# Cosine attention, Fourier mixing and a feed-forward block: a lone tile first, other homes for one batch's raw rows, and a new priority table

## The chip, the cores and the metric

The kernel runs on one core of a Trainium2 chip. The metric is the device time of one execution in microseconds. The kernel before takes 575.24 us (median of three runs, 574.73 to 575.60).

## The reference

Eight batches of twelve heads, 448 tokens, 64 numbers a head. Queries and keys are divided by their norms, the scores by tau, the softmax weights the values. Then a real-valued two-dimensional Fourier transform over tokens and over the 768 channels is added to its input, each row is normalised, and a feed-forward block of 768 to 3072 to 768 with a relu is added:

```python
def _attn_ref(q, k, v, tau) -> np.ndarray:
    q_n = q / (np.linalg.norm(q, axis=-1, keepdims=True) + 1e-06)
    k_n = k / (np.linalg.norm(k, axis=-1, keepdims=True) + 1e-06)
    scores = np.matmul(q_n, k_n.transpose(0, 1, 3, 2)) / tau
    scores = scores - np.max(scores, axis=-1, keepdims=True)
    attn = np.exp(scores)
    attn = attn / (np.sum(attn, axis=-1, keepdims=True) + 1e-09)
    return np.matmul(attn, v).astype(np.float32)

def _moe_ref(x, w_ch1, w_ch2) -> np.ndarray:
    X = np.fft.fft(x, axis=1)
    X = np.fft.fft(X, axis=2)
    mixed = np.real(X).astype(np.float32)
    u = x + mixed
    mu = np.mean(u, axis=-1, keepdims=True)
    var = np.mean((u - mu) ** 2, axis=-1, keepdims=True)
    un = (u - mu) / np.sqrt(var + 1e-06)
    ch = np.maximum(un @ w_ch1, 0.0) @ w_ch2
    return (u + ch).astype(np.float32)
```

All inputs and the output are float32; q, k and v are batch by head by token by channel.

## The kernel before

**Work and its names.** Everything below is written as a list of operations, each with a name that ends in its batch. For a batch the loads `ld_k`, `ld_q` (and `ld_t`, the last 64 tokens) bring raw rows from DRAM; `sq` squares them, `ss` sums the squares, `ln` and `nrm` make the norms of a group of heads (an Ln and an Exp on ACT, L1173 and L1175), `sc` scales the rows, and they reach the TensorE's layout (batches 0 and 1 through TensorE transposes `tk`, `tq`, `tt` and copies; the others through DMA transposes `tr`, L1393). `qk` are the score products (L1464 and L1477), `ex` the exponentials on ACT (L1442), `pv` the products with V (L1495 for the last tokens, L1501), `x` the division. `f`, `fs`, `te` and `fd` belong to the Fourier transform, `ba`, `bs`, `ln2` and `rs` to the row norm (`bs` is L1769), `tru` brings the normed rows to TensorE's layout by DMA (L1800; in batch 0 `tn` by TensorE, L1789, and `eu` copies them out of PSUM, L1797). `h0` to `h23` are the 24 column blocks of the first feed-forward product (L1864), `relu` takes four blocks of one tile or two of a pair out of PSUM (L1880), and `y` or `m1` to `m7` are the second product (L2008), `fin` the additions behind it, `st` the store.

**Tiles.** Rows of the feed-forward block are worked in tiles of 128. Even batches have three tiles, odd ones four (28 in all), and two tiles that follow each other make a pair whose second product is done with seven block products instead of eight (L2073 on: sums and differences of the two weights and of the two hidden tiles). `ONES` on L27 names the two tiles that stay single: (batch, tile) (0, 0) and (2, 2). Batch 7 and part of batch 6 multiply the first weight in the same way (`ups`, L1959, with the weight sums on VectorE at L1901, L1912 and L1944).

**Order.** Each operation gets a priority, to which a table `SHIFT` adds a number of its own, and a table `HOME` ties some operations to an engine. `Plan.schedule` (L675 on) then plays the program through with costs from tables, always starting the operation with the lowest priority among those that could start first, and so fixes one list of instructions for each engine. On the chip each engine runs its list strictly in that order, waiting where a row has a wait; the DMA issues of SP and of POOL stand in those lists too. `Plan.fill` then puts warm-up products (six matmuls on data of no interest, L2258) where the schedule has holes on TensorE: with the identity up to the first `h`, with a piece of W1 from there to 20 us ahead of the planned end, the latter only where the schedule is thin.

**Batch 1's raw rows.** `first_norm` (L1179) loads the rows of batches 0 and 1. Batch 0's stand in the tile buffers TX. Batch 1's come in two groups of three head pairs: `ld_k0_1`, `ld_t0_1`, `ld_q0_1` and `ld_k1_1`, `ld_t1_1`, `ld_q1_1`; a K or Q load is 576 KB, a t load is two of 96 KB. They all lie where W2 will be (`W2b[:, 10:24]`), and the squares of the first group's Q lie there as well (`W2b[:, 7:10]`, square `sqQ0_1`); W2's pieces therefore wait for the operations that read them (L2235 to L2241). Nothing in W2b is old, so these loads wait only for the first piece of W1 (gate, `self.w[0]`).

**Head of the program.** W1 comes on POOL's DMA queue in seven pieces and W2 behind it in twelve, each piece behind the landing of an earlier one (L1145). The first tile of batch 0 is single: 24 blocks `h` of 6 matmuls with 128 columns, in groups of four that share one of two PSUM banks, so `h8` can start once `relu0` has read the bank of `h0` to `h3`.

Of the kernel before, what the change touches and what calls it, by code (L numbers as in the profile page):

```python
# [26 lines left out]
ONES = ((0, 0), (2, 2))  # L27
# [55 lines left out]
    "iota": {0: -4743.9411}, "iotak": {0: -3749.0012}, "cst": {0: 2295.738}, "iotad": {0: 1504.4864}, "rown": {0: 3564.9514},  # L83
    "tqd": {0: 5876.6502, 1: 5614.4443}, "trd": {0: 5875.7288}, "tpd": {0: -1558.5233, 1: 550.4848}, "tad": {0: 4737.392},
    "tqs": {0: 4545.6213, 1: 5636.9779}, "trs": {0: 4448.6198}, "tps": {0: -162.6304, 1: -1607.3824}, "tas": {0: -178.9521}, "ktd0": {0: 1975.3204},
# [4 lines left out]
    "mask": {0: 35657.0228}, "sinp": {0: 48649.0823}, "half": {0: 440.6683, 1: 3500.6271}, "sinn": {0: 17464.9799}, "ldt": {0: 44319.0778},  # L90
# [2228 lines left out]
```

## Time and profile before

| what | value |
|---|---|
| median of three runs | 575.24 us (574.73 to 575.60) |
| the profiled execution | 575.0 us, span 573.2 us |
| TensorE (PE) busy | 553.7 us, 97% of the span |
| VectorE (DVE), ScalarE (ACT), GpSimd (POOL) busy | 434.0, 392.9, 224.4 us |
| granted TensorE clock | 1.00 |
| DMA | 62.19 MB, 108 GB/s on average |

The profiled execution is 575.0 us long, 1.8 us more than its span. "Busy" counts the time in which an engine runs an instruction; TensorE's warm-up products count as busy, though they do nothing for the result. The page cuts the span into 40 slices of 14.3 us.

### The profile page before, as it was taken

The page shows a single profiled execution, that of the slowest core. Times are in us where ns is not written, and L with a number is a line of the kernel's source. Part 1 is how long each engine was busy: PE and PEld are TensorE (multiplying, and loading weights), DVE is VectorE, ACT ScalarE, POOL GpSimd, SP SyncE. Part 2 cuts the span into 40 slices and gives each one's busy share as a digit, 9 for nine tenths or more (in the row PEclk, how much of TensorE's full clock was granted, in tenths as well). Part 3 has the DMA queues.
Part 4 walks back from the last instruction along what each step waited for, and adds up shares of the span by engine and source line. Part 5 has one row for each costly group of instructions (what it writes and reads, how often), then busy time and mean ns, then how long its engine had stood idle before and what let it go on. Part 6 is the DMA issues. An engine that isn't in the chain of part 4 may idle for free.

```text
span 573.2 us, 16025 instructions
## 1 busy us (share of the span) xinstructions
PE 553.7 (97%) x6616; PEld 432.9 (76%) x6616; DVE 434.0 (76%) x923; ACT 392.9 (69%) x734; POOL 224.4 (39%) x332
## 2 busy tenths in 40 slices
PE   3899999999999899999999999999999999999998
PEld 2578887686787687878778688687886876959695
DVE  9889868987469867986789669965679379886353
ACT  7998976576776885578648886686665761948171
POOL 8522414356328542702380736443524003041304
PEclk9999999999999999999999999999999999999999
DMA  9999997976359645963496569461691200132001
GB/s 213 170 241 202 164 195 108 163 173 111 111 82 113 158 88 111 155 145 70 95 157 76 99 138 125 105 140 23 136 87 27 72 2 17 42 48 66 24 34 56
DMA packets 183945, 62.19 MB, mean 108 GB/s; under 512 B 166688, under 2 KB 181664, under 8 KB 183872
## 3 DMA queue, kind: packets, MB, share of 16 engines
q1 hardware_dynamic: 129824, 38.35, 35.2%
q0 software_dynamic: 54048, 22.81, 32.1%
q8 instruction: 52, 0.85, 0.6%
q14 instruction: 21, 0.17, 0.1%
HBM read 51.90 MB, written 11.01 MB: 110 GB/s over the span
## 4 chain that ended last, share of the span: by engine, by line
PE 78%; DVE 8%; ACT 6%; issue 3%; POOL 2%; DMA 2%; SPq 1%; POOLq 0%; DVEq 0%; ACTq 0%
PE PS L1864 28%; PE PS L2008 26%; PE PS L1959 7%; PE PS L1501 5%; PE PS L1464 5%; PE PS L1495 2%; PE PS L1477 1%; DMA TX<-in_q_dram 1%; ACT F L1769 1%; POOL QH L1387 1%; DVE F L1547 1%; POOL OUTB L2034 1%; PE PS L1685 1%; DVE OUTB L2045 1%; DVE X L1521 1%
## 5 line engine op out<-in xcount | busy, mean ns | idle before, releaser
L1864 PE MATMUL PS<-UNT,W1b 128*128 128x256 bf16 (+1 forms) x1728 | 185.4, 264 | 0.3 <-DVE UNT L1797 0.2
L1442 ACT ACTIVATE E<-PS 128x900 bf16<-128x900 f32 (+1 forms) x192 | 148.7, 827 | 30.3 <-PE PS L1464 24.3
L1864 PEld LDWEIGHTS PS<-UNT,W1b 128*128 128x128 bf16 x1728 | 153.4, 98 | 20.1 <-issue 1.9
L2008 PE MATMUL PS<-W2b,HQ 128*128 128x384 bf16 x720 | 124.9, 326 | 0.0
L1387 POOL TENSOR_TENSOR QH<-STG,SM 128x256 bf16<-128x256 f32 x126 | 84.4, 696 | 86.8 <-DVE SM L1177 65.0
L2008 PEld LDWEIGHTS PS<-W2b,HQ 128*128 128x128 bf16 x720 | 68.8, 98 | 43.1 <-issue 0.4
L2034 POOL TENSOR_TENSOR OUTB<-OUTB,U 128x192 f32<-128x192 f32 x72 | 51.6, 737 | 118.2 <-ACT OUTB L2029 115.6
L2008 PE MATMUL PS<-TX,HQ 128*128 128x384 bf16 (+2 forms) x444 | 76.4, 322 | 0.9 <-DVE OUTB L2045 0.5
L1880 ACT ACTIVATE HQ<-PS 128x512 bf16<-128x512 f32 x86 | 51.2, 595 | 28.8 <-PE PS L1864 27.6
L2108 DVE TENSOR_TENSOR HQ<-HQ 128x1536 bf16<-128x1536 bf16 (+1 forms) x73 | 54.1, 744 | 12.2 <-ACT HQ L1880 7.0
L2008 PEld LDWEIGHTS PS<-TX,HQ 128*128 128x128 bf16 x444 | 41.5, 98 | 27.9 <-DVE OUTB L2045 2.4
L1374 ACT ACTIVATE QH<-STG 128x384 f32<-128x384 f32 x84 | 43.1, 519 | 17.6 <-DVE SM L1376 11.6
L1376 DVE TENSOR_REDUCE SM<-QH 128x6 f32<-128x384 f32 x84 | 45.3, 544 | 11.3 <-ACT QH L1374 11.0
L1501 PE MATMUL PS<-VB,E 128*128 128x65 bf16 x1152 | 51.6, 193 | 0.0
L2067 POOL DMA_INDIRECT out_dram<-OUTB,IDX x21 | 23.7, 1127 | 69.2 <-DVE OUTB L2045 43.4
L1501 PEld LDWEIGHTS PS<-VB,E 128*128 128x128 bf16 x1152 | 47.8, 97 | 1.3
L1880 DVE TENSOR_SCALAR HQ<-PS 128x512 bf16<-128x512 f32 x40 | 27.4, 685 | 23.9 <-PE PS L1864 23.8
L1495 PE MATMUL PS<-VZ,E 128*128 128x130 bf16 x192 | 41.6, 219 | 2.0 <-issue 1.9
L1727 DVE SCALAR_TENSOR_TENSOR U<-ACG,X 128x768 bf16<-128x768 f32 (+4 forms) x39 | 39.5, 1023 | 0.9
L2029 ACT ACTIVATE OUTB<-PS 128x384 f32<-128x384 f32 x36 | 17.7, 491 | 32.2 <-PE PS L2008 29.4
L1464 PE MATMUL PS<-QK 64*128 64x225 bf16 (+2 forms) x864 | 39.2, 227 | 0.5 <-ACT QK L1290 0.5
L1464 PEld LDWEIGHTS PS<-QK 64*128 64x128 bf16 x864 | 25.6, 95 | 13.2 <-issue 6.6
(195 smaller groups left out, 784.5 us busy)
## 6 DMA issues: line engine op xcount, KB each, us to landing
STG<-in_q_dram SPq DMA_DIRECT2D x18, 384.0 KB, 3.9
STG<-in_k_dram SPq DMA_DIRECT2D x18, 384.0 KB, 3.9
VB<-in_v_dram POOLq DMA_DIRECT2D x24, 192.0 KB, 6.4
W2b<-in_moe_w_ch_dram POOLq DMA_DIRECT2D x12, 384.0 KB, 7.4
W1b<-in_moe_w_ch_dram POOLq DMA_DIRECT2D x5, 768.0 KB, 14.7
out_dram<-OUTB SPq DMA_DIRECT2D x7, 384.0 KB, 2.7
W2b<-in_k_dram SPq DMA_DIRECT2D x2, 576.0 KB, 9.1
W2b<-in_q_dram SPq DMA_DIRECT2D x2, 576.0 KB, 15.9
```

Of the source, the lines that this page charges most:

```text
L1374: P.add("act", lambda a, sq=sq, src=buf[:, w * x:w * x + w]: a.activation(sq, src, ACTF.Square), t_act(w), pr, f"sq{i}_{b}", reads=bn, wri ...
L1376: P.add("dve", lambda v, o=SS[:, i, H // ns * x:H // ns * (x + 1)], sq=sq: v.tensor_reduce(o, sq.rearrange("p (h d) -> p h d", d=DH), AX.X ...
L1387: r = v.tensor_tensor(v3(qh)[:, h:h + 4], v3(buf)[:, h:h + 4], RN[:, i, h:h + 4].unsqueeze(2).to_broadcast((128, 4, DH)), AluOp.mult)
L1442: return a.activation(o, self.PS[:, bk:bk + nc_, 0:SQ2], ACTF.Exp, scale=1.0 / self.tau)
L1464: i = pe.matmul(self.PS[:, bk + h, c0:c0 + n], self.KT[r, jj, kt * 128:(kt + 1) * 128], self.QT[r, jj, cols], start=True, stop=True)
L1495: r = pe.matmul(o, st(6), self.VZ[:, j, :], start=not split, stop=(split and i == 0), skip_group_check=True)
L1501: r = pe.matmul(o[:, 65 * h:65 * h + 65], st(2 * kt + h), self.VB[:, kt, 2 * j + h, :], start=(split and i == h == kt == 0), stop=((not sp ...
L1864: r = pe.matmul(self.PS[:, bk, x * n:(x + 1) * n], self.W1b[:, j, ft * 128:(ft + 1) * 128], self.UNT[:, j, cs], start=(j == 0), stop=(j == ...
L1880: return e.activation(o, i, ACTF.Relu) if e is self.nc.scalar else e.tensor_relu(o, i)
L2008: r = pe.matmul(self.PS[:, bk, 0:n], lhs(f), rhs(f), start=(start and f == 0), stop=(stop and f == NF // 2 - 1), skip_group_check=True)
L2034: r = g.tensor_tensor(self.OUTB[:, ob, xs], self.OUTB[:, ob, xs], self.U[:, ut, xs], AluOp.add)
L2108: P.add("dve", lambda v: v.tensor_tensor(cs(o), cs(a), cs(bq), op), 0.16 + 0.3 * len(ks), -0.5, f"{nm}{ks[0]}_{b}", reads=rd, writes=[x fo ...
```

## The change

1. `ONES` is ((0, 0), (2, 0)): batch 2's first tile is the single one and goes first, and its other two make the pair behind it.
2. Batch 1's raw rows no longer lie in W2's home. The first group and the second group's K go to the buffer of batch 0's raw rows (TX, `self.tf[:, 1536:9216]`), the second group's Q and t to the staging buffers STG; the squares of `sqQ0_1` go to the buffer E1 of the exponentials. The loads now also wait for the operations that read batch 0's raw rows (the table `told`), and two of batch 2's loads wait for readers of batch 1's rows in STG. W2's pieces no longer wait for batch 1's rows.
3. The second stretch of warm-up products ends 12 us behind the first `h` instead of 20 us ahead of the planned end.
4. Every number of `SHIFT` and `HOME` is new, so the lists of all engines are in another order.

The program's lists hold the same products otherwise. The diff, of which the tables are left out:

```diff
--- before.py
+++ after.py
@@ -24,7 +24,7 @@
 TF = 4
-ONES = ((0, 0), (2, 2))
+ONES = ((0, 0), (2, 0))
 HELD = (5, 3)
@@ -80,538 +80,556 @@
 SHIFT = {
-    "iota": {0: -4743.9411}, "iotak": {0: -3749.0012}, "cst": {0: 2295.738}, "iotad": {0: 1504.4864}, "rown": {0: 3564.9514},
...
@@ -1198,11 +1216,12 @@
             gate = []
         else:
             cuts = ((0, 3), (3, 6))
-            hf = flat(self.W2b[:, 10:24, :]).bitcast(F32)
-            sw = flat(self.W2b[:, 7:10, :]).bitcast(F32)
+            hf = self.tf[:, 1536:9216].bitcast(F32)
+            sf = flat(self.STG[:])
+            sw = self.E[1][:, 0:2304].bitcast(F32)
             sqs = [[ob[:, 0:1152], sw, ob[:, 1152:1536]], [ob[:, 0:1152], ob[:, 0:1152], ob[:, 1152:1536]]]
             o0 = ["OUT0", "OUT0b", "OUT1", "OUT0d", "OUT1d"]
-            sqn = [[o0, ["SQW"], ["OUT1b", "OUT1d"]], [o0, o0, ["OUT1b", "OUT1d"]]]
+            sqn = [[o0, ["SQW"] + [f"E1_{c}" for c in range(7)], ["OUT1b", "OUT1d"]], [o0, o0, ["OUT1b", "OUT1d"]]]
             qhb = [(qf, 0), (self.tf, 0), (self.tf, 1152)]
             raw = ["Sk0_0", "Sk1_0"]
             qhn = [[["QH0", "QH1x"], raw + ["QM"], raw + ["QMt"]], [["QH1", "QH2"], ["QM"], ["QMt"]]]
@@ -1213,9 +1232,10 @@
         for g, (a, z) in enumerate(cuts):
             n = z - a
             o, ja = 2688 * (a // 3), a % 3
-            K, Q, R = [hf[:, o + x + y * ja:o + x + y * (ja + n)] for x, y in ((0, 384), (1152, 384), (2304, 128))]
+            K, Q, R = [(sf[:, DM + x - 1152 + y * ja:DM + x - 1152 + y * (ja + n)] if b and g and x else hf[:, o + x + y * ja:o + x + y * (ja + n)])
+                       for x, y in ((0, 384), (1152, 384), (2304, 128))]
             nt = (3, 0, 3)[g] if b == 0 else n
-            R3 = hf[:, o + 2304 + 128 * ja:o + 2304 + 128 * (ja + nt)]
+            R3 = R if b else hf[:, o + 2304 + 128 * ja:o + 2304 + 128 * (ja + nt)]
             L = [("k", [(heads(K, n), self.heads(self.k, b, 2 * a, 2 * n, 0, 3, 128, 192))], 0.64 * n),
                  ("q", [(heads(Q, n), self.heads(self.q, b, 2 * a, 2 * n, 0, 3, 128, 192))], 0.64 * n)]
             if nt:
@@ -1225,12 +1245,15 @@
             parts.append((g, a, n, nt, R3, L, [("K", K, [f"Sk{g}_{b}"]), ("Q", Q, [f"Sq{g}_{b}"]), ("T", R, [f"St{gt}_{b}"])]))
         sc, ID = [], self.ID
         for g, a, n, nt, R3, L, ps in parts:
+            told = {}
+            if b:
+                told = {"k": ["Sk1_0", "Sq0_0", "Sq1_0"], "q": ["Sq1_0", "St0_0", "Sk2_0"], "t": ["Sk2_0"]} if g == 0 else {"k": ["Sk2_0", "Sq2_0"]}
             for nm, dm, sv in L:
                 def fn(sy, sem, dm=dm):
                     for dst, src in dm:
                         sy.dma_start(dst, src).then_inc(sem, 16)
                 self.loads.append(P.add("sp", fn, (0.36 if b else 0.55) * len(dm), pg[g], f"ld_{nm}{g}_{b}", writes=[f"S{nm}{g}_{b}"],
-                                        dma=(f"lh{g}{nm}{b}", 16 * len(dm)), serve=sv, after=gate, order=self.loads[-1:] if b == 0 else ()))
+                                        dma=(f"lh{g}{nm}{b}", 16 * len(dm)), serve=sv, after=gate + [r for x in told.get(nm, ()) for r in P.rd[x]], order=self.loads[-1:] if b == 0 else ()))
                 if (b, g, nm) == (0, 1, "k"):
                     self.vgate = self.loads[-1]
             red, rn = [], [[f"RN_{a + j}{i}" for j in range(n)] for i in range(3)]
@@ -1363,7 +1386,7 @@
                 def fn(sy, sem, dm=dm):
                     for dst, src in dm:
                         sy.dma_start(dst, src).then_inc(sem, 16)
-                self.loads.append(P.add("sp", fn, 0.36 * len(dm), pr, f"ld_{kind}{t}_{b}", writes=bn,
+                self.loads.append(P.add("sp", fn, 0.36 * len(dm), pr, f"ld_{kind}{t}_{b}", writes=bn + ({1: ["Sq1_1"], 2: ["Sq1_1", "St1_1"]}.get(s, []) if b == 2 else []),
                                         dma=(key, 16 * len(dm)), after=gate, serve=1.75))
                 r = self.qh_next % 6
                 self.qh_next += 1
@@ -2183,7 +2206,7 @@
         P = self.P
         B = lambda r, c, k: self.W2b[:, 12 * r + 4 * k:12 * r + 4 * k + 4, 384 * c:384 * c + 384]
         X = lambda x, k: self.TX[:, x, 4 * k:4 * k + 4, :]
-        old = ["ID", "rowf", "CSp", "QLt", "QLu", "QLu_1", "QLv", "QLv_1", "QLv_2", "QM", "QMt"] + [f"S{x}{g}_0" for x in "kqt" for g in range(3)] + [
+        old = ["ID", "rowf", "CSp", "QLt", "QLu", "QLu_1", "QLv", "QLv_1", "QLv_2", "QM", "QMt"] + [f"S{x}{g}_0" for x in "kqt" for g in range(3)] + ["Sk0_1", "Sq0_1", "St0_1", "Sk1_1"] + [
             f"QM{t}_{j}" for t in ("", "t") for j in (1, 2)]
         w = lambda r, k: [f"W2_{6 * r + 2 * k + x}" for x in range(2)]
         for k in range(3):
@@ -2235,10 +2258,6 @@
 
                 for c in range(3):
                     self.w[12 + c].deps.update(self.ssk)
-                for c in (3, 4):
-                    self.w[12 + c].deps.add(self.sqw)
-                for c in range(5, 12):
-                    self.w[12 + c].deps.update(self.raw1[3] + (self.raw1[4] if c > 7 else []))
             if b == self.nb - 2:
                 self.s1 = []
                 self.wsums()
@@ -2260,7 +2279,7 @@
                 return fn
             return make
         self.P.fill(7.5, first, self.id_op, warm(self.ID))
-        self.P.fill(first, self.est - 20.0, self.id_op, warm(self.W1b[:, 0, 0:128]), 0.75)
+        self.P.fill(first, first + 12.0, self.id_op, warm(self.W1b[:, 0, 0:128]), 0.75)
         self.P.emit(self.nc, self.es)
         self.es.close()
 
```

**Three places in the lists.** On SP, the loads of batch 1's rows, which stand right behind those of batch 0 (TX<- rows there). A 128x6x192 row is a K or Q load of 576 KB, the two 64x6x64 rows are one t load, d_W1_0 is the landing of W1's first piece, and prog_act, prog_dve and prog_pool stand for a point that ACT, DVE or POOL must have reached. Before:

```order
L1231 DMA W2b<-in_k_dram 128x6x192 [waits d_W1_0]
L1231 DMA W2b<-in_q_dram 64x6x64
L1231 DMA W2b<-in_k_dram 64x6x64
L1231 DMA W2b<-in_k_dram 128x6x192
L1231 DMA W2b<-in_q_dram 128x6x192 x2
L1231 DMA W2b<-in_q_dram 64x6x64
L1231 DMA W2b<-in_k_dram 64x6x64
```

and now:

```order
L1254 DMA STG<-in_q_dram 64x6x64 [waits d_W1_0]
L1254 DMA STG<-in_k_dram 64x6x64
L1254 DMA STG<-in_q_dram 128x6x192
L1254 DMA TX<-in_k_dram 128x6x192 [waits prog_act,prog_dve]
L1254 DMA TX<-in_q_dram 64x6x64 [waits prog_pool,prog_act,prog_dve]
L1254 DMA TX<-in_k_dram 64x6x64
L1254 DMA TX<-in_q_dram 128x6x192
L1254 DMA TX<-in_k_dram 128x6x192 [waits prog_dve,prog_act]
```

Before, the order is k0, t0, k1, q1, q0, t1; now it is t1, q1, k0, t0, q0, k1, so the second group's K moved from third to last, and three of the loads wait for engines.

On ACT, the rows around the first feed-forward products. The 128x1152 squares are `sqK1_1` and `sqQ0_1` (d_lh1k1 and d_lh0q1 are the landings of k1 and q0), UNT<-PS is `eu00_0`, the copy that the first `h` needs, and 128x512 is a `relu`. Before:

```order
L1249 ACTIVATE OUTB<-W2b 128x1152 [waits prog_dve,prog_act,d_lh1k1]
L1769 ACTIVATE F,MV<-U,MV 128x768 [waits prog_dve]
L1797 ACTIVATE UNT<-PS 128x3x128 [waits prog_pe]
L1772 ACTIVATE MV<-MV 128x1 [waits prog_act]
L2206 ACTIVATE CS<-CS 97x2x96 [waits prog_dve]
L1249 ACTIVATE W2b<-W2b 128x1152 [waits d_lh0q1]
L1774 ACTIVATE MV<-MV 128x1 [waits prog_act]
L1880 ACTIVATE TX<-PS 128x512 [waits prog_pe] x2
L1173 ACTIVATE SM<-SM,MV 128x42 [waits prog_dve]
L1175 ACTIVATE SM<-SM 128x42 [waits prog_act]
```

and now:

```order
L1272 ACTIVATE E<-TX 128x1152 [waits d_lh0q1]
L1792 ACTIVATE F,MV<-U,MV 128x768 [waits prog_dve]
L1795 ACTIVATE MV<-MV 128x1 [waits prog_act]
L1820 ACTIVATE UNT<-PS 128x3x128 [waits prog_pe]
L1797 ACTIVATE MV<-MV 128x1 [waits prog_act]
L1272 ACTIVATE OUTB<-TX 128x1152 [waits d_lh1k1]
L1191 ACTIVATE SM<-SM,MV 128x42 [waits prog_dve]
L1193 ACTIVATE SM<-SM 128x42 [waits prog_act]
L2229 ACTIVATE CS<-CS 97x2x96 [waits prog_dve]
L1903 ACTIVATE TX<-PS 128x512 [waits prog_pe]
```

`sqQ0_1` moved from behind `eu00_0` to ahead of it, and `sqK1_1`, the norms of the first group (128x42) and one small copy now stand ahead of the first `relu`.

On TensorE, the place where batch 2's feed-forward block begins and batch 3's first head pair is scored. L2008 (now L2031) are the last products of batch 1's block, 128x225 the scores of batch 3's first pair, 128x130 and 128x65 its products with V, and 128x128 with W1b the blocks `h` of a single tile. Before:

```order
L1464 MATMUL PS<-QK 128x225 x12
L2008 MATMUL PS<-TX,HQ 128x384 x12
L1477 MATMUL PS<-QK,KTD 128x225 x2
L1495 MATMUL PS<-VZ,E 128x130
L1501 MATMUL PS<-VB,E 128x65 x6
```

and now:

```order
L1487 MATMUL PS<-QK 128x225 x12
L2031 MATMUL PS<-TX,HQ 128x384 x12
L1500 MATMUL PS<-QK,KTD 128x225 x2
L1887 MATMUL PS<-UNT,W1b 128x128 x24
L1518 MATMUL PS<-VZ,E 128x130
L1524 MATMUL PS<-VB,E 128x65 x6
```

Four blocks `h` of the single tile, 24 matmuls, came between the scores and the products with V.

More of the change, by code (lines that the diff above doesn't have):

```diff
@@ L82 @@
 SHIFT = {
[L83 to L85 removed]
[4 rows of a table removed]
[L90 removed]
[510 rows of a table removed]
+    "iota": {0: 988.1999}, "iotak": {0: 2280.7807}, "cst": {0: 2561.5506}, "iotad": {0: 3021.5255}, "rown": {0: -5211.4485},
@@ L601 @@
+    "tqd": {0: 7923.068, 1: 60.9428}, "trd": {0: -5147.3146}, "tpd": {0: 13287.2598, 1: 11.7343}, "tad": {0: 13314.1014},
+    "tqs": {0: -5211.7732, 1: 826.4541}, "trs": {0: 55.947}, "tps": {0: -2188.111, 1: -5124.9522}, "tas": {0: 4226.7561}, "ktd0": {0: 3088.7005},
[4 rows of a table added]
+    "mask": {0: 38931.3111}, "sinp": {0: 41339.771}, "half": {0: 3552.1202, 1: 17376.0333}, "sinn": {0: 10202.0605}, "ldt": {0: 53454.3582},
[507 rows of a table added]
 }
 HOME = {
-    "tqd": {0: "dve", 1: "dve"}, "trd": {0: "dve"}, "tas": {0: "act"}, "sinp": {0: "dve"}, "half": {0: "pool", 1: "act"}, "sqK0_0": {0: "act"},
@@ L613 @@
-    "ek1_1": {0: "act"}, "ek2_1": {0: "dve"}, "eq2_1": {0: "act"}, "relu0_0": {0: "act"}, "relu4_0": {0: "act"}, "relu8_0": {0: "dve"},
-    "relu12_0": {0: "act"}, "relu16_0": {0: "act"}
+    "tqd": {0: "dve", 1: "dve"}, "trd": {0: "dve"}, "tad": {0: "dve"}, "tas": {0: "act"}, "sinp": {0: "dve"}, "half": {0: "pool", 1: "act"},
+    "sinn": {0: "act"}, "sqK0_0": {0: "act"}, "sqQ0_0": {0: "act"}, "sqT0_0": {0: "dve"}, "scK0_0": {0: "dve"}, "scQ0_0": {0: "dve"},
+    "scT0_0": {0: "dve"}, "ek0_0": {0: "act"}, "eq0_0": {0: "act"}, "et0_0": {0: "dve", 1: "act"}, "sqK1_0": {0: "dve"}, "sqQ1_0": {0: "act"},
@@ new lines @@
+    "relu10_0": {0: "dve"}, "relu14_0": {0: "act"}, "relu18_0": {0: "dve"}, "relu22_0": {0: "act"}, "ktd2": {0: "dve"}, "gc1_2": {0: "act"},
+    "relu0_1": {0: "act"}, "relu12_1": {0: "act"}, "relu14_1": {0: "act", 1: "dve"}, "relu20_1": {0: "act"}, "relu22_1": {0: "act", 1: "act"},
+    "relu16_1": {1: "dve"}, "relu6_1": {1: "act"}, "ktd3": {1: "act"}, "te0_3": {0: "act"}, "ct0": {0: "dve"}, "ct3": {0: "act"},
+    "relu4_2": {0: "dve"}, "relu16_2": {0: "act", 1: "dve"}, "relu20_2": {0: "dve"}, "relu2_2": {0: "act"}, "relu6_2": {0: "act"},
@@ new lines @@
+    "te0_6": {0: "act"}, "te1_6": {0: "dve"}, "relu0_5": {0: "dve", 1: "dve"}, "relu12_5": {0: "dve"}, "relu16_5": {0: "dve", 1: "act"},
+    "relu6_5": {0: "act", 1: "act"}, "relu18_5": {0: "act"}, "relu8_5": {0: "act"}, "relu10_5": {0: "act"}, "relu14_5": {1: "act"},
+    "ktd7": {0: "act", 1: "act"}, "gc1_7": {0: "act"}, "te0_7": {0: "act"}, "relu0_6": {0: "act"}, "relu12_6": {0: "act"}, "relu2_6": {0: "dve"},
+    "relu14_6": {0: "dve"}, "relu4_6": {0: "dve"}, "relu16_6": {0: "act"}, "relu6_6": {0: "dve"}, "relu18_6": {0: "dve"}, "relu8_6": {0: "dve"},
@@ L615 @@
+    "relu10_6": {0: "act"}, "relu22_6": {0: "act"}, "c2r1_6": {0: "dve"}, "c41_6": {1: "act", 2: "act"}, "c1r1_6": {3: "act"}, "c3r1_6": {3: "act"},
+    "c1r0_7": {1: "act"}, "c2r0_7": {1: "act"}, "c3r0_7": {2: "dve"}, "c40_7": {1: "dve"}, "c1r2_7": {0: "dve", 1: "act"}, "c2r2_7": {0: "dve"},
+    "c42_7": {0: "dve", 1: "act", 2: "dve"}
 }
```

20 lines of the change are left out of this document (12 added, 8 removed), and 1031 rows, old and new, of tables (HOME, SHIFT).

## The prediction

> **What bounds the kernel now.** I read the page's first two parts, then TensorE's waits, then a table of stretches. In the first fence the last three rows are the 40 slices of TensorE and DMA; in the waits the numbers are total us, times and longest.
>
> ```profile
> span 573.2 us, 16025 instructions
> PE 553.7 (97%) x6616; PEld 432.9 (76%) x6616; DVE 434.0 (76%) x923; ACT 392.9 (69%) x734; POOL 224.4 (39%) x332
> PE   3899999999999899999999999999999999999998
> DMA  9999997976359645963496569461691200132001
> ...
> PE PS L2258 <- DVE HQ L1249: 7.6, 1, 7.6
> PE PS L1495 <- issue: 1.9, 2, 1.5
> PE PS L1959 <- DVE HQ L1979: 0.8, 1, 0.8
> PE PS L1959 <- DMA UNT<-F: 0.5, 1, 0.5
> ```
>
> TensorE bounds everything from the second slice on. Its idle time is 573.2 - 553.7 = 19.5 us; 7.6 us of it lie ahead of its first product, and no later wait is longer than 1.5 us. So the change can win little behind the head: the three longest of them hold 1.5 + 0.8 + 0.5 = 2.8 us. The next table gives, for each stretch, its length, the busy us of PE, PEld, DVE, ACT and POOL, the granted clock, the DMA share and GB/s.
>
> ```profile
> 22.00:34.00 12.00, 10.82 (x179) 7.52 (x177) 9.57 (x21) 11.46 (x19) 6.81 (x8) 1.00 1.22 241
> 34.00:48.00 14.00, 13.36 (x192) 10.91 (x188) 12.30 (x39) 13.04 (x19) 1.52 (x2) 1.00 1.18 226
> 48.00:60.00 12.00, 10.90 (x172) 9.95 (x173) 11.74 (x38) 10.34 (x28) 6.05 (x8) 1.00 1.42 184
> 60.00:100.00 40.00, 40.00 (x509) 32.41 (x510) 31.16 (x66) 30.52 (x52) 12.35 (x17) 1.00 1.04 156
> ```
>
> Up to 60 us four things are tight together (ACT is 93 to 96% busy until 48 us, the DMA engines are full); from there TensorE is without a hole. What the change does to the head therefore ends in one number, the time at which that solid stretch begins.
>
> **The head: loads.** The moved rows come on SP's queue while W1 comes on POOL's, both full. These are SP's issues and how long three of them took to land (the large q loads issued at 26.61 and 29.4, and the last t):
>
> ```profile
> 26.61 5.76 SPq L1231 DMA_DIRECT2D W2b<-in_q_dram  x3
> 32.41 5.61 SPq L1231 DMA_DIRECT2D W2b<-in_k_dram  x1
> ...
> L1231 SPq DMA_DIRECT2D W2b<-in_q_dram x2: 1430/1464/1497, 29.4 to 30.9; - x2
> ...
> W2b<-in_q_dram SPq DMA_DIRECT2D x1, 576.0 KB, 14.3
> ...
> W2b<-in_q_dram SPq DMA_DIRECT2D x1, 576.0 KB, 17.4
> ...
> W2b<-in_k_dram SPq DMA_DIRECT2D x1, 96.0 KB, 19.5
> ```
>
> So q1 landed at 26.61 + 14.3 = 40.9, q0 at 29.4 + 17.4 = 46.8 (5.9 us behind q1 in the same queue), and the last byte of batch 1 at 32.41 + 19.5 = 51.9. The same bytes in another order end at the same time if the queue never runs dry. In the new order k1 is last: it lands at about **51.9** (51.4 if the small t loads at the front overlap better), and q0, one large load ahead of the end (5.9 us by these rows, more beside a W1 piece), at 45 to 46.
>
> **The head: ACT.** What stands on ACT there, from the timeline (start, length):
>
> ```profile
> 46.53 0.94 ACT L1769 ACTIVATE F<-U,MV 128x768 bf16<-128x768 bf16 x1 [0.20 <-DVE MV L1765]
> 47.55 0.49 ACT L1797 ACTIVATE UNT<-PS 128x384 bf16<-128x384 f32 x1
> 48.12 0.35 ACT L2206 ACTIVATE CS<-CS 97x192 bf16<-97x192 bf16 x1
> 48.38 1.15 ACT L1249 ACTIVATE W2b<-W2b 128x1152 f32<-128x1152 f32 x1
> 49.72 0.60 ACT L1880 ACTIVATE TX<-PS 128x512 bf16<-128x512 f32 x1
> 51.55 0.32 ACT L1173 ACTIVATE SM<-SM,MV 128x42 f32<-128x42 f32 x1
> 51.91 0.24 ACT L1175 ACTIVATE SM<-SM 128x42 f32<-128x42 f32 x1
> ```
>
> Now `sqQ0_1` waits for q0 ahead of `bs` (L1769) and `eu00`. With q0 at 45.5 the square (1.15) ends at 46.65, and `bs` starts 0.1 later than the 46.53 of its row; with q0 at 45 nothing is late, at 46 it is 0.6. One small operation more stands ahead of the copy, about the 0.24 of the row at 51.91. I take the first `h` **0.3 us later**, at 48.5 (bounds 0 and +0.9).
>
> The other move costs more. `relu0` sits behind `sqK1_1`, hence behind k1: 51.4 to 51.9, then 1.15 + 0.32 + 0.24 + 0.35 + 0.60 = 2.66 by the rows, of which about 0.1 a seam overlaps (48.12 + 0.35 is 48.47 and the next row starts at 48.38): **53.7 to 54.2**. Behind it on ACT stand all later relus and norms of the head. TensorE, in its rows:
>
> ```profile
> 48.17 5.53 PE L1864 MATMUL PS<-UNT,W1b 128*128 128x128 bf16 x96 [0.18 <-DVE UNT L1797]
> 54.14 0.84 PE L2258 MATMUL PS<-W1b 128*128 128x128 bf16 x12 [0.44 <-DVE CS L2207]
> 54.98 1.51 PE L1864 MATMUL PS<-UNT,W1b 128*128 128x128 bf16 x24
> 57.04 0.49 PE L2258 MATMUL PS<-W1b 128*128 128x128 bf16 x6
> ```
>
> Before, 96 matmuls (16 blocks) ran in 5.53 us without a hole, 0.058 us each. Now 48 of them (`h0` to `h7`) end at 48.5 + 2.8 = 51.3 and TensorE then stands until `relu0` is done, **2.4 to 2.9 us**. Before, however, the stretch from 48 to 60 lost 12.00 - 10.90 = 1.1 us to idling and about 1.0 us to three warm-up groups (0.84 - 0.17 + 0.33; those groups are gone now, which alone is worth nothing, since they filled waits). By the time TensorE is past `h23`, batch 1's transposes have long had their data, and these 2.1 us need not be lost again. The head's net is 0.3 + 2.4 - 2.1 = +0.6 with k1 at 51.4 and +1.1 with it at 51.9. I take **+0.6**, since the tight queue also serves W1's pieces and its last 0.5 us may go to them, with bounds -1.5 (rival a) and +2.5 (late end of k1, and most of the old losses paid again).
>
> W2's pieces are freed from waits. That is nothing: the table shows DMA over its full share until 100 us, so an earlier issue only queues. The staging waits of two loads of batch 2 are nothing as well, since in that stretch TensorE is at 40.00 of 40.00 with ACT and DVE at 76 to 78%, cover of several us; if that cover were gone a late row would cost its own lateness.
>
> **Batch 2's lone tile first.** The place is the 1.5 us wait of the second waits row:
>
> ```profile
> 192.53 0.36 PE L1477 MATMUL PS<-QK,KTD 128*128 128x225 bf16 x2
> 194.36 0.22 PE L1495 MATMUL PS<-VZ,E 128*128 128x130 bf16 x1 [1.47 <-issue]
> ...
> 191.19 2.96 ACT L1442 ACTIVATE E<-PS 128x900 bf16<-128x900 f32 x4
> ...
> 190.07 3.03 SPq L1800 DMA_TRANSPOSE UNT<-F  x2
> ```
>
> The products with V wait for four exponentials, done at 191.19 + 2.96 = 194.15. Now 24 matmuls of the lone tile stand in that hole: 24 x 0.058 = 1.4 us, nearly all of the 1.47. They need only one tile's rows, whose transpose is among the two issued from 190.07. Against it, a norm pair now stands ahead of these exponentials on ACT (0.32 + 0.24 by the rows of such a pair above), which leaves a rest of 0.1 to 0.6 us. I take **-0.9** (-1.5 to -0.3; a transpose that comes after 193 would make it nothing). The count of products stays the same, and the pair now has four more blocks ahead of its own rows.
>
> **The rest of the new order.** Two later holes are touched:
>
> ```profile
> 485.19 0.54 DVE L2045 TENSOR_TENSOR OUTB<-PS,U 128x384 f32<-128x384 f32 x1
> 487.65 1.18 PE L1959 MATMUL PS<-KTD,STG 128*128 128x128 bf16 x18 [0.80 <-DVE HQ L1979]
> ...
> 515.01 2.17 PE L1959 MATMUL PS<-UNT,W1b 128*128 128x128 bf16 x36 [0.54 <-DMA UNT<-F]
> ...
> 508.70 10.63 SPq L1800 DMA_TRANSPOSE UNT<-F  x4
> ```
>
> At 487 VectorE works through the weight sums; one addition like that of 485.19 (0.54) moved behind the awaited copy, another came ahead by less: **-0.25** (0 to -0.5). At 515 four transposes stand 10.63 / 4 = 2.66 apart, and the two that are awaited moved from second and third to first and second: **-0.3** (0 to -0.54). All other holes are under 0.5 us; I put the remaining swaps at 0, with bounds of -0.5 and +1.0, since a table can both close and open such holes and TensorE has no slack to hide a new one.
>
> **Sum** against the profiled 575.0: +0.6 - 0.9 - 0.25 - 0.3 = -0.85, thus 574.15. That execution lies 0.24 under the runs' median of 575.24 and inside their spread of 574.73 to 575.60, so I leave the sum where it is: **574.2**.
>
> **Rivals.** (a) *k1 and q0 land earlier.* For it: the rate of SP's queue is not a constant (q0 came 5.9 us behind q1, while q1 itself came 14.3 us behind its issue with two loads ahead of it), and W1's pieces, which share the engines, may stand elsewhere. Against it: DMA is full, and the same bytes take the same time. If k1 is there by 49.5, `relu0` ends at 51.9, TensorE's hole is 0.6 instead of 2.4, the head wins 1.8 on the forecast, and the time is 572.4.
>
> (b) *SP's queue runs dry.* Three loads wait for the scaling of batch 0's rows, which POOL ends at about 29.5:
>
> ```profile
> 28.64 0.86 POOL L1276 TENSOR_TENSOR QH<-TX,SM 128x384 bf16<-128x384 f32 x1
> ```
>
> The loads ahead of them (the t halves and q1) keep the queue busy for some 9 to 11 us from its start, to about 33, as k0, t0 and k1 did before. If the last reader, on ACT or DVE, ends after about 31.5 (2 us ahead for the issue), each us more delays k1, `sqK1_1`, `relu0` and `h8` by a us. At 34 that is 2.5 us on the chain: 576.7. POOL's row speaks against it, the new order of DVE and POOL leaves it open.
>
> (c) *The holes are not closed but moved*: the gains at 192, 487 and 515 come to 0.3 (their lower bounds) while the head pays its 0.6: 575.3, no change.
>
> (d) TensorE's clock. The longest hole that this trace shows behind the start is 1.47 us, with the clock at 1.00 in every stretch; the new one of 2.4 to 2.9 us has no warm-up products in it. If the clock then ran at half for as long as the hole lasted, the lost work would be about 2.7 / 2 = 1.4 us: 575.6. The Trainium skill, "TensorE: Matmul & The Clock Gate", Part 1 (The HAM clock gate), says that a free-running window of about 3.4 us in which the array is idle halves its clock; no run here shows such a window yet. By that rule a hole of 2.7 us costs only itself, and one that k1 makes 0.7 us longer would cost the clock too.
>
> **How the numbers follow.** Forecast 0.42, (a) 0.18, (b) 0.20, (c) 0.16, (d) 0.04. This kernel's runs can tell about 0.2%, 1.15 us: faster is under 574.09, slower over 576.39. The forecast's own range is 573.2 to 575.2 and lies on both sides of the first line, about as much under it as over: 0.22 faster and 0.20 same. (a) adds 0.18 faster; (b) 0.15 slower and 0.05 same, where it decides late; (c) 0.02 faster, 0.11 same, 0.03 slower; (d) 0.02 same, 0.02 slower: faster 0.42, same 0.38, slower 0.20. The range takes in (a) and (b) up to their prices: 572.0 to 576.8.
>
> **What would show it.** k1's landing near 51.9 and q0's near 45.5; a hole of 2.4 to 2.9 us on TensorE behind the eighth block, and the first products with V of batch 1 about 0.6 us later than the 70.86 of this row:
>
> ```profile
> 70.86 0.22 PE L1495 MATMUL PS<-VZ,E 128*128 128x130 bf16 x1
> ```
>
> The wait ahead of batch 3's first products with V at 0.6 us or less, the one at 487 at 0.8 or less, the one at 515 near 0.2. Wrong would be: no hole behind `h7`, a k1 that lands before 50 or after 53, or a new wait over 0.6 us behind 60 us.

## The result, and the profile after

The changed kernel takes 580.13 us (median of four runs, 579.35 to 580.37) against 575.42 us (574.73 to 575.67) for the kernel before in the same job: a ratio of 1.008, with a 95% interval of 1.0064 to 1.0096. It is slower by 4.7 us; the forecast was 574.2 us, and its range ended at 576.8. The profiled execution took 580.37 us.

The first two parts of the page after:

```profile
span 578.6 us, 15969 instructions
PE 553.6 (96%) x6586; PEld 434.8 (75%) x6586; DVE 435.5 (75%) x929; ACT 386.8 (67%) x727; POOL 224.5 (39%) x333
PE   3896899999999999999999999999999998999997
...
PEclk9699999999999999999999999999999999999999
```

TensorE is as busy as before (553.6 us against 553.7), so the 5.4 us of span are idle time. The slices put most of it into the fourth and the fifth (9 and 9 before, now 6 and 8), from about 43 to 72 us. The table of stretches (length; busy us of PE, PEld, DVE, ACT, POOL; clock; DMA share; GB/s) of the kernel after:

```profile
34.00:48.00 14.00, 13.48 (x202) 10.98 (x198) 12.58 (x39) 12.22 (x17) 1.53 (x2) 1.00 1.20 214
48.00:60.00 12.00, 7.39 (x121) 6.72 (x120) 7.12 (x23) 6.83 (x15) 5.80 (x8) 1.00 1.36 194
60.00:100.00 40.00, 38.30 (x529) 32.20 (x527) 32.41 (x72) 33.01 (x61) 7.15 (x11) 1.00 0.87 137
```

From 48 to 60 us TensorE lost 10.90 - 7.39 = 3.5 us, from 60 to 100 another 40.00 - 38.30 = 1.7 us. TensorE's waits of the kernel after name the places (total us, times, longest):

```profile
PE PS L1887 <- ACT TX L1903: 2.9, 1, 2.9
PE PS L2031 <- DVE OUTB L2068: 2.2, 2, 1.6
PE PS L1887 <- ACT MV L1797: 1.6, 1, 1.6
...
PE PS L1887 <- DVE TX L1903: 1.1, 1, 1.1
```

L1887 are the blocks `h`, so three of these four waits lie in the head: 1.6 + 2.9 + 1.1 = 5.6 us. The timeline of TensorE after, at these three and at the first products with V of batch 1:

```profile
51.57 2.84 PE L1887 MATMUL PS<-UNT,W1b 128*128 128x128 bf16 x48 [1.57 <-ACT MV L1797]
57.33 2.85 PE L1887 MATMUL PS<-UNT,W1b 128*128 128x128 bf16 x48 [2.92 <-ACT TX L1903]
61.26 1.18 PE L1887 MATMUL PS<-UNT,W1b 128*128 128x128 bf16 x18 [1.07 <-DVE TX L1903]
...
76.84 0.22 PE L1518 MATMUL PS<-VZ,E 128*128 128x130 bf16 x1
```

That last row stood at 70.86 before. So 5.98 us were lost up to there, and 0.58 us of it came back in the 500 us behind it (578.6 - 76.84 = 501.76, before 573.2 - 70.86 = 502.34). ACT's timeline after shows what TensorE waited for:

```profile
48.64 1.16 ACT L1272 ACTIVATE E<-TX 128x1152 f32<-128x1152 f32 x1 [2.02 <-DMA TX<-in_q_dram]
...
54.88 1.16 ACT L1272 ACTIVATE OUTB<-TX 128x1152 f32<-128x1152 f32 x1 [3.37 <-DMA TX<-in_k_dram]
...
56.70 0.58 ACT L1903 ACTIVATE TX<-PS 128x512 bf16<-128x512 f32 x1
```

ACT waited 2.02 us for q0 and 3.37 us for k1; `relu0` began at 56.70 (before 49.72). Both loads are late. SP's issues after, then POOL's rows of the same time, and how long the loads took to land (a view by windows of issue):

```profile
23.67 1.20 SPq L1254 DMA_DIRECT2D TX<-in_k_dram  x1
31.95 0.60 SPq L1254 DMA_DIRECT2D TX<-in_q_dram  x1
32.60 0.67 SPq L1254 DMA_DIRECT2D TX<-in_k_dram  x1
33.33 0.91 SPq L1254 DMA_DIRECT2D TX<-in_q_dram  x1
34.33 2.47 SPq L1254 DMA_DIRECT2D TX<-in_k_dram  x1
...
29.31 1.70 POOL L1172 DMA_DIRECT2D W1b<-in_moe_w_ch_dram  x2 [0.55 <-POOL QH L1299]
31.02 0.85 POOL L1299 TENSOR_TENSOR QH<-TX,SM 128x384 bf16<-128x384 f32 x1
...
TX<-in_k_dram SPq DMA_DIRECT2D x1, 576.0 KB, 8.7
TX<-in_q_dram SPq DMA_DIRECT2D x1, 96.0 KB, 7.5
TX<-in_k_dram SPq DMA_DIRECT2D x1, 576.0 KB, 20.5
```

The load t0 waits for `scK4_0`, the scaling of batch 0's K rows on POOL that read the buffer t0 overwrites. In POOL's new list that operation stands behind two issues of W1 pieces (1.70 us) and ends at 31.02 + 0.85 = 31.87; t0 is issued at 31.95. The load ahead of it, k0, had landed at 23.67 + 8.7 = 32.4, only 0.4 us behind t0's issue. By these times SP's queue ran empty until t0's first bytes came, while W1's pieces, issued by POOL from 29.31 on, were there for the DMA engines to move. The small t0 took 7.5 us, and k1 landed at 34.33 + 20.5 = 54.8, against 51.9 for the last byte before.

### The profile page after: what moved, and what is told of

Read it like the earlier page. It is cut to its first block, busy times and chain, and to the rows that moved or that the text cites. A ratio compares the mean times of both kernels' runs of the same rounds, so it can differ in the third digit from the quotient of the medians.

```text
span 578.6 us, 15969 instructions
## 1 busy us (share of the span) xinstructions
PE 553.6 (96%) x6586; PEld 434.8 (75%) x6586; DVE 435.5 (75%) x929; ACT 386.8 (67%) x727; POOL 224.5 (39%) x333
## 4 chain that ended last, share of the span: by engine, by line
PE 61%; DVE 4%; issue 1%; ACT 1%; POOLq 0%; ACTq 0%; DVEq 0%
PE PS L2031 22%; PE PS L1887 20%; PE PS L1982 7%; PE PS L1487 4%; PE PS L1524 4%; PE PS L1518 1%; PE PS L1500 1%; PE PS L1651 1%; PE PS L1708 1%; DVE F L1570 1%; DVE STG L1924 0%; DVE OUTB L2068 0%; DVE X L1544 0%; DVE ACG L1563 0%; PE PS L1705 0%
## 5 line engine op out<-in xcount | busy, mean ns | idle before, releaser
L1887 PE MATMUL PS<-UNT,W1b 128*128 128x256 bf16 (+1 forms) x1728 | 186.2, 264 | 5.9 <-ACT TX L1903 2.9
L1887 PEld LDWEIGHTS PS<-UNT,W1b 128*128 128x128 bf16 x1728 | 153.5, 98 | 26.0 <-ACT TX L1903 3.1
L2031 PE MATMUL PS<-W2b,HQ 128*128 128x384 bf16 x720 | 125.6, 326 | 0.4 <-ACT OUTB L2052 0.4
L2031 PEld LDWEIGHTS PS<-W2b,HQ 128*128 128x128 bf16 x720 | 68.7, 98 | 43.4 <-issue 1.1
L2057 POOL TENSOR_TENSOR OUTB<-OUTB,U 128x192 f32<-128x192 f32 x72 | 50.3, 718 | 113.2 <-ACT OUTB L2052 100.9
L2031 PE MATMUL PS<-TX,HQ 128*128 128x384 bf16 (+2 forms) x444 | 76.4, 322 | 2.2 <-DVE OUTB L2068 2.2
L2031 PEld LDWEIGHTS PS<-TX,HQ 128*128 128x128 bf16 x444 | 41.7, 98 | 28.7 <-DVE OUTB L2068 3.2
L1524 PE MATMUL PS<-VB,E 128*128 128x65 bf16 x1152 | 52.8, 194 | 0.0
```

The source lines that it names most:

```text
L1524: r = pe.matmul(o[:, 65 * h:65 * h + 65], st(2 * kt + h), self.VB[:, kt, 2 * j + h, :], start=(split and i == h == kt == 0), stop=((not sp ...
L1887: r = pe.matmul(self.PS[:, bk, x * n:(x + 1) * n], self.W1b[:, j, ft * 128:(ft + 1) * 128], self.UNT[:, j, cs], start=(j == 0), stop=(j == ...
L2031: r = pe.matmul(self.PS[:, bk, 0:n], lhs(f), rhs(f), start=(start and f == 0), stop=(stop and f == NF // 2 - 1), skip_group_check=True)
L2057: r = g.tensor_tensor(self.OUTB[:, ob, xs], self.OUTB[:, ob, xs], self.U[:, ut, xs], AluOp.add)
```

## The experiments

Each kernel is timed beside the kernel before (575.39 to 575.58 us in the jobs). None leaves out a part of the computation; the warm-up products that some add or drop compute nothing that is used. Several move one operation within an engine's list after the order is fixed: `move(engine, what, where, behind)`.

**The homes.** The changed kernel with its lists, but with batch 1's rows in W2's home and their loads waiting for W1's first piece alone, as before:

```diff
-            hf = self.tf[:, 1536:9216].bitcast(F32)
-            sw = self.E[1][:, 0:2304].bitcast(F32)
+            hf = flat(self.W2b[:, 10:24, :]).bitcast(F32)
+            sw = flat(self.W2b[:, 7:10, :]).bitcast(F32)
...
+        for op in self.P.ops:
+            if op.name in ("ld_k0_1", "ld_q0_1", "ld_t0_1", "ld_k1_1", "ld_q1_1", "ld_t1_1"):
+                op.deps = {self.w[0]}
+        (and W2's pieces wait for the readers of these rows again)
```

> The changed kernel with batch 1's rows back in W2's home, so that their loads wait for W1's first piece alone; the order of every list is the changed one. If the waits for batch 0's readers emptied SP's queue, the loads are issued from 22 to 31 without a gap, the last K load lands at about 52, q0 near 46, and the time is 577 to 577.7. If the queue only lost to W1's and W2's pieces, which now stand earlier, the last landing stays near 54.5 and the time at 579.5 to 580.3.

Measured: 575.85 us (ratio 1.0005, 0.9995 to 1.0015), so 4.3 of the 4.7 us are gone, more than either expectation had. Its SP rows and the first products with V of batch 1:

```profile
22.79 1.63 SPq L1253 DMA_DIRECT2D W2b<-in_k_dram  x1
24.47 3.51 SPq L1253 DMA_DIRECT2D W2b<-in_q_dram  x1
...
70.90 0.22 PE L1517 MATMUL PS<-VZ,E 128*128 128x130 bf16 x1
```

t0 is issued at 24.47 instead of 31.95, and the head ends at 70.90 where before had 70.86. k1 was issued at 29.35 and took 13.3 us: it landed at 42.7, where about 52 was expected. The loss needs the new homes; the new order of the lists by itself hardly costs.

**The scaling on POOL.** The changed kernel with one operation moved ahead of the W1 issues:

```diff
         self.est = self.P.schedule()
+        move("pool", [("scK4_0", 0)], ("W1w_4", 0), False)
```

> The changed kernel with one scaling of batch 0's rows (scK4_0) moved on POOL ahead of two issues of W1's pieces, where it stood before; homes, waits and all other lists are the changed ones. If that scaling is what SP's loads wait for, the load t0 is issued near 29.7 instead of 31.9, the last K load lands some 5 to 9 us earlier than 54.9, and the time is 576.3 to 577.8. If another reader of batch 0's rows or the queue's share binds, t0 moves by less than 0.5 us and the time stays over 579.

Measured: 575.17 us (0.9994, 0.9982 to 1.0006): the whole loss is gone with the homes as the change put them. That is below the 576.3 to 577.8 that were expected if the scaling was what the loads waited for; and it is no faster than the kernel before, so the gain that the prediction saw in the rest of the change does not show either. The profiled execution was this kernel's slowest (577.68 us) and began about 1.2 us late, but shows the mechanism. Its SP issues and landings, and TensorE at the `h`:

```profile
24.91 1.04 SPq L1254 DMA_DIRECT2D TX<-in_k_dram  x1
31.11 0.60 SPq L1254 DMA_DIRECT2D TX<-in_q_dram  x1
...
33.15 1.65 SPq L1254 DMA_DIRECT2D TX<-in_k_dram  x1
...
TX<-in_k_dram SPq DMA_DIRECT2D x1, 576.0 KB, 8.9
TX<-in_q_dram SPq DMA_DIRECT2D x1, 96.0 KB, 3.0
TX<-in_k_dram SPq DMA_DIRECT2D x1, 576.0 KB, 17.7
...
31.57 2.52 POOL L1172 DMA_DIRECT2D W1b<-in_moe_w_ch_dram  x3 [0.55 <-POOL QH L1299]
...
51.45 5.52 PE L1887 MATMUL PS<-UNT,W1b 128*128 128x128 bf16 x96
```

Here t0 is issued 0.5 us ahead of the next W1 pieces, in the change 2.6 us behind them. k0 lands at 24.91 + 8.9 = 33.8, 2.7 us behind t0's issue (0.4 in the change); t0 takes 3.0 us instead of 7.5, k1 lands at 50.85, and the 96 matmuls run without a hole. From k0's landing to k1's it is 17.0 us, in the changed kernel 22.4. The windows of 30 to 34 us, first after, then this kernel (last two columns: DMA share and GB/s):

```profile
30.00:32.00 2.00, 1.95 (x41) 1.40 (x40) 1.57 (x6) 1.97 (x4) 1.85 (x3) 1.00 1.07 206
32.00:34.00 2.00, 1.95 (x36) 1.56 (x37) 1.08 (x2) 2.00 (x3) 0.87 (x1) 1.00 1.19 194
```

```profile
30.00:32.00 2.00, 2.00 (x37) 1.48 (x33) 1.93 (x5) 1.70 (x4) 1.38 (x3) 1.00 1.05 310
32.00:34.00 2.00, 2.00 (x43) 1.68 (x41) 1.58 (x5) 1.88 (x3) 2.00 (x3) 1.00 0.61 101
```

With SP's large loads nearly alone the engines move 310 GB/s; with W1's pieces in it is 200 in all. The windows also show that there is a gap with the scaling moved: from 32 to 34 us the engines are at 0.61 of their share. That gap costs nothing that can be measured. In the change the engines are busy in these windows, at a DMA share of 1.07 and 1.19, with W1's pieces issued 2.6 us ahead of t0.

**The scaling's place without the wait.** The kernel before with its scaling put behind the W1 issues, as the changed list has it (`move("pool", [("scK4_0", 0)], ("W1w_6", 0))`):

> The kernel before with the same scaling moved on POOL behind a second issue of a W1 piece, where the changed kernel has it; the homes are the old ones, so that no load waits for it. If the scaling's place costs through SP's loads alone, the time stays at 575.0 to 575.9. If the late scaling costs by itself (its transpose, batch 0's fifth head pair) or the earlier W1 piece takes the engines, it is 577 or more.

Measured: 575.53 us (1.0001, 0.9989 to 1.0012). As far as these times can tell, the place on POOL costs only where SP's loads wait for it.

**The order on ACT.** The changed kernel with the squares of q0 and k1 moved behind what TensorE waits for:

```diff
+        move("act", [("sqQ0_1", 0)], ("eu00_0", 0))
+        move("act", [("relu0_0", 0), ("relu4_0", 0)], ("rs0_0", 0))
+        move("act", [("sqK1_1", 0)], ("relu12_0", 0))
```

> The changed kernel with another order on ACT alone: the square of batch 1's Q behind the copy that the first h needs, the first two relus ahead of the norms, and the square of the last K load behind the fourth relu. Landings stay as they are (48.6 and 54.9). If it is the place of the two squares on ACT that turns late landings into holes, the waits of 1.6, 2.9 and about 1 us ahead of h0, h8 and h16 go, less what the transposes of batch 1 then wait for: 576.5 to 577.5. If the norms that need those rows bind anyway, the holes only move behind h23 and the time is 579 or more.

Measured: 579.16 us (1.0063, 1.0049 to 1.0077): 1.0 us of the 4.7. Its TensorE rows:

```profile
50.71 5.52 PE L1887 MATMUL PS<-UNT,W1b 128*128 128x128 bf16 x96
58.75 1.18 PE L1887 MATMUL PS<-UNT,W1b 128*128 128x128 bf16 x18 [2.52 <-DVE TX L1903]
```

The hole behind the eighth block is gone and stands behind the sixteenth instead. This kernel can't say what ACT's order costs with late loads, because the moves open a hole of their own, as the next kernel shows.

**Both.** The same three moves on top of the moved scaling:

> The changed kernel with the one scaling moved on POOL and, besides, ACT's order mended (square of batch 1's Q behind the copy for the first h, the first two relus ahead of the norms, the square of the last K load behind the fourth relu). If the squares' place still costs once the loads are early, the rest of the waits ahead of h0, h8 and h16 go and the time is 573.2 to 574.4. If the early loads make the place harmless, it is 574.8 to 575.5, as with the scaling alone.

Measured: 578.94 us (1.0062, 1.0049 to 1.0075), which is 3.8 us more than with the scaling alone, where at most 575.5 had been expected. VectorE and TensorE in its timeline:

```profile
50.77 1.35 DVE L1276 TENSOR_REDUCE SM<-E 128x18 f32<-128x1152 f32 x1 [1.24 <-ACT E L1272]
...
57.21 0.69 DVE L1903 TENSOR_SCALAR TX<-PS 128x512 bf16<-128x512 f32 x1
...
57.96 1.18 PE L1887 MATMUL PS<-UNT,W1b 128*128 128x128 bf16 x18 [2.60 <-DVE TX L1903]
```

The square of q0, now late, holds VectorE's sum of it for 1.24 us, everything behind it on VectorE follows, and a relu there comes at 57.21, for which TensorE waits 2.60 us. The loads are early here (k1 landed at 31.48 + 17.8 = 49.3), and the hole is the same as the 2.52 us of the kernel with the three moves alone, where VectorE waited 1.23 us for that square too. So both holes come from the square's later place, not from late rows. ACT's order in the change fits loads that are on time: with them it costs nothing (575.17 us with the scaling alone), and with late ones it is where their lateness reaches TensorE.

**The clock in the first 25 us.** A second suspect came from the page: the granted clock is 0.6 in the second slice after. The change leaves TensorE without warm-up groups from 12 to 22.6 us. Windows of after, and two like operations (three transposes) of before and after:

```profile
14.00:25.00 11.00, 8.29 (x82) 6.35 (x83) 8.05 (x19) 9.75 (x19) 3.72 (x8) 0.54 2.10 155
...
17.81 0.82 PE L1334 MATMUL PS<-TX,QH 128*128 128x128 bf16 x3
```

```profile
17.26 0.50 PE L1311 MATMUL PS<-TX,QH 128*128 128x128 bf16 x3
```

The clock was 0.54 there and the transposes took 0.82 us instead of 0.50. So two kernels: the changed one with twelve warm-up groups more (`warm_before("tk0_0", 2)` and seven other places between 12 and 23 us), and the one before without its own:

```diff
+        q, k = self.P.order["pe"], next(i for i, o in enumerate(self.P.order["pe"]) if o.name == "tk0_0")
+        z = next(i for i, o in enumerate(q) if o.name == "qk10_0")
+        self.P.order["pe"] = q[:k] + [o for o in q[k:z] if o.name != "warm"] + q[z:]
```

> The changed kernel with twelve more warm-up groups (six matmuls each) on TensorE between 12 and 23 us, all else in its place. If the half clock of 14 to 25 us is what delays the first exponentials, the granted clock is 1.00 throughout, ACT's last exponential of batch 0 ends near 37.6 instead of 39.1, batch 0's last scaling on POOL ends about 1.2 us earlier, the last K load of batch 1 lands near 53.5 instead of 54.9, and the time is 577.5 to 578.5. If the clock was harmless because ACT and the loads set the pace there, the time stays at 579.7 to 580.4.

> The kernel before without the six warm-up groups between its first and its second head pair's scores (12 to 20 us), all else in its place. If missing warm-up products alone bring the half clock, the granted clock falls to 0.5 for about 10 us from 15 us on, and the time rises by 1.0 to 1.7, to 576.3 to 577. If the real products keep the clock up or ACT hides it, the time stays within 0.4 of 575.3.

Measured: with the groups 580.79 us (1.009, 1.0074 to 1.0105), no better than the change and over both expected ranges, although TensorE then ran at full rate (three transposes 0.49 us at 18.24); ACT's first exponential came at 17.62 (17.17 in the change), and t0 was still issued only at 32.84. The kernel before without its groups takes 577.96 us (1.0039, 1.0025 to 1.0053), 2.6 us more, where at most 577 was expected. In it the same transposes took

```profile
18.23 0.85 PE L1311 MATMUL PS<-TX,QH 128*128 128x128 bf16 x3
```

The surest evidence is the kernel with the scaling moved: it has no groups there either, three transposes take 0.82 us at 19.02, and its time is 575.17 us. So the slow stretch is real, and leaving out the groups costs in the old order, but it is not what the change lost by.

**The lists of before and after, put together.** In these kernels a table names, engine by engine, the order of operations over a stretch of the plan, and the planner may start only the next of it:

```diff
+            if pin[op] != (e, len(self.order[e])):
+                continue
```

All but the last kernel of this part have the homes and the waits of the kernel before; the first two and the last have batch 2's lone tile first, the others behind its pair. *Tail*: before's lists up to 100 us of the plan and the change's order behind. *Lone tile*: the change's order from 100 to 262 us only. *Late*: the change's order from 348 us on only. *Head*: the change's order up to 100 us, before's to 348, the change's behind; and the *head without its start*, the same with before's lists for the first 22 us.

> The kernel before with its own lists, homes and warm-up products up to 100 us of the plan, and from there the changed kernel's order, the lone tile first included. If everything that the change loses is lost in the head, this shows the rest alone: the holes at 192, 487 and 515 gone, new ones of 0.5 to 1.8 at 193, 296 and 486, in sum 0.6 less than before, 574.5 to 575.0. If the rest of the order gained only because a late head gave its producers time, the time is 575.2 to 576.

> The kernel before with the lone tile of batch 2 first: its own lists up to 100 us of the plan, the changed order from there to 262 us (batch 2's feed-forward block), its own order again behind that. If the four blocks h fill the hole of 1.5 us at 192 as forecast, the first products with V of batch 3 no longer wait more than 0.6 us and the time is 573.9 to 574.7 (a seam of up to 0.5 at 262 us included). If the hole only moves to the second products of batch 1 or to the pair's rows, it is 575.0 to 575.8.

> The kernel before with the changed order from 348 us of the plan on alone (batches 5 to 7). If the reorder there is worth what the traces show, the hole of 0.8 at 487 and of 0.5 at 515 go and one of 1.8 at 486 comes in place of 0.5 at 481: within 0.4 of the time before, 574.8 to 575.4. If the new hole at 486 came from the late head, it stays at 0.5 and the time is 574.0 to 574.5.

Measured: tail 576.50 us (1.0021, 1.0009 to 1.0032), lone tile 575.16 (0.9997, 0.9986 to 1.0007), late 574.74 (0.9989, 0.9979 to 0.9999). The tail is slower than both of its expected ranges; the lone tile lies in the range for a hole that only moves. In the lone-tile kernel TensorE's timeline shows the hole closed that the prediction spoke of, and another one opened 5 us ahead of it:

```profile
189.60 2.11 PE L2172 MATMUL PS<-W2b,HQ 128*128 128x384 bf16 x12 [0.82 <-DVE U L1891]
...
194.29 0.36 PE L1641 MATMUL PS<-QK,KTD 128*128 128x225 bf16 x2
194.49 1.50 PE L2028 MATMUL PS<-UNT,W1b 128*128 128x128 bf16 x24
195.83 0.22 PE L1659 MATMUL PS<-VZ,E 128*128 128x130 bf16 x1
```

The tail as a whole loses 1.1 us on before's head, though its last third gains about 0.6.

> A version put together from both: homes, lone tile and code of the kernel before; its own lists up to 22 us of the plan, the changed order from there to 100, its own to 348, the changed order behind. If the late copies of the first 22 us and the half clock are the rest of the head's loss, batch 0's exponentials end near 37 and the time is 573.0 to 574.2. If the head's start does not matter once the loads are early, it equals its companion without the old first 22 us.

> The companion: homes, lone tile and code of the kernel before, the changed order up to 100 us of the plan, the old one to 348, the changed one behind. Batch 0's exponentials end near 38 to 39. If the head's start counts, the time is 0.6 to 1.5 above the companion's, 574.2 to 575.4; if not, both are the same within 0.3.

Measured: head without its start 575.80 us (1.0005, 0.9992 to 1.0018), head 574.93 (0.9993, 0.9981 to 1.0004). q0 landed at 42.9 in the first and at 36.5 in the second, but the intervals overlap: with loads on time, neither the change's first 22 us nor an earlier q0 costs or wins anything that can be measured.

> The companion kernel of before (old homes, changed order to 100 us, old to 348, changed behind) with the scaling scK4_0 ahead of two issues of W1's pieces on POOL. No load waits for it, so only W1's pieces move, some 0.9 us later. If W1's later issue gave the loads more of the DMA engines, the last K load lands at 42 to 43 in nearly every run and the time is 574.0 to 574.6; if the wait was all, it stays at 574.7 to 575.4, as without the move.

This is the head kernel with the scaling moved ahead of the W1 issues as above; no load waits for it there. Measured: 575.84 us (1.0010, 0.9999 to 1.0022), no gain, and above both expected ranges. W1's issues being later is thus not what the move on POOL won; the wait was.

> The changed kernel (new homes, lone tile first) with the scaling moved on POOL, and the old order between 262 and 348 us of the plan. If the changed order loses about 1 us in that stretch (waits of 0.8 and 0.5 at 294 and 298), the time is 574.0 to 574.6, below the 575.2 of the scaling alone. If that difference came from something else, it is 575.0 to 575.6.

This is the changed kernel with the scaling moved and before's order from 262 to 348 us. Measured: 575.81 us (1.0009, 0.9998 to 1.0019). The expectation failed: two holes near 295 and 300 us did shrink, but a wait of 1.03 us opened at 119 us, outside the stretch that was changed, and the time did not fall. In which stretch the tail's 1.1 us lie is not settled.

## Why the prediction was wrong, point by point

**The step that failed** is rival (b)'s condition: "Three loads wait for the scaling of batch 0's rows, which POOL ends at about 29.5." The 29.5 came from before's row at 28.64. In the change's list that operation stands behind two W1 issues, which last 1.70 us, and it ended at 31.87, past the 31.5 from which the rival was said to decide. The rival was the right mechanism, with a chance of 0.20. The chance should have followed the new list of the engine that is waited for, and the prediction looked at the lists of SP, ACT and TensorE only.

**Its price was mis-sized too**: 2.5 us, by a us of delay for each us of waiting. The wait ran 0.4 us over its limit and cost about 5 us (after against the kernel with the scaling moved: 580.13 - 575.17). In the profiles the way from k0's landing to k1's grew by 5.4 us (22.4 against 17.0). That the wait is the cause is shown by the moved scaling, by the homes (only the waits and places of the rows changed) and by the two controls without a wait (575.53 and 575.84 us). How its price divides between t0's later issue and its place behind W1's pieces was not separated. t0 was issued 31.95 - 23.67 = 8.28 us behind k0 in the change and 31.11 - 24.91 = 6.20 us with the scaling moved, so 2.1 us of the price may be the later issue alone; the rest may be W1's pieces, which were issued ahead of t0. The last kernel above, which has the scaling moved as well and starts as early as the change does (k0 issued at 23.95), had t0 issued at 29.93 and k1 landed at 32.03 + 18.0 = 50.0, 4.8 us ahead of the change.

**"The same bytes in another order end at the same time if the queue never runs dry"**: the condition was named and did not hold. The sentence itself fails too: in the homes kernel, with the new order and no wait for an engine, k1 landed at 42.7, nine us ahead of the last byte before, and in the head kernel without its start, with the same order of loads and the same homes, at 30.18 + 18.8 = 49.0. When the last load lands is thus not given by the bytes alone; what sets it is open. With the new homes q0 was forecast at 45 to 46 and landed at 33.33 + 15.3 = 48.6; k1 at 51.4 to 51.9 and landed at 54.8.

**The head on ACT and TensorE** came as worked out, only later: the order of squares, small operations and relus gives `relu0`'s end at 57.28 = 54.8 + 2.5 (forecast: 2.3, which is 2.66 less what overlaps). The hole behind the eighth block was forecast at 2.4 to 2.9 us and is 2.92, by chance near, since the first `h` was late as well: it began at 51.57, 1.57 us of it waiting behind q0's square, where 48.5 was forecast. "These 2.1 us need not be lost again" was too hopeful with such rows: 1.07 us were lost at 61.26.

**W2's waits, staging waits at nothing**: no wait of TensorE after has a release by them, and the kernel with the scaling moved, which keeps both edits, is at 0.9994 of before.

**Lone tile, -0.9**: the closing of the hole is confirmed, in the change too (the 24 matmuls stand there and the products with V follow without a wait). Its worth was not: the lone-tile stretch alone gives 575.16 against 575.42, -0.26 with an interval that takes in zero; a hole of 0.82 us opened ahead of batch 1's last products.

**487 and 515, -0.55 together, other swaps at 0**: both holes are gone in the change, but ahead of 488 a new one stands:

```profile
488.26 2.12 PE L2031 MATMUL PS<-TX,HQ 128*128 128x384 bf16 x12 [1.60 <-DVE OUTB L2068]
```

Before, that place lost 0.46 us. The late stretch as a whole still wins about 0.6 (by its interval 0.06 to 1.2), near its term. All that lies behind the head was forecast at -1.45 and is -0.58 in the profile.

**The rivals.** (a) early landings: only kernels with the old homes had them (q0 at 36.5 and k1 at 42.7 in the homes kernel), and there they were worth no time. (c) holes that move: true of the lone tile and of ACT's order. (d) the clock: with a hole of 2.92 us the window from 48 to 60 us still shows 1.00, so it fell; the 48 matmuls behind the hole took 2.85 us, those ahead of it 2.84. That hole is shorter than the idle window of about 3.4 us that the Trainium skill, "TensorE: Matmul & The Clock Gate", Part 1, asks for, and the trace agrees with it there. Overlooked altogether was the start of the head, where the clock did halve; the kernel with the scaling moved says that it decided nothing here.
